# Table, signal and cross-term sums by accumulating transfers, the last 64 channels on both partition halves, and the squares' doublings moved into the transform rows

## The chip, the cores and the metric

The kernel runs on one core of a Trainium2 chip. The core has five engines, each with a queue of its own that it works off in order: TensorE (PE, matmuls and, overlapped with them, weight loads, PEld), VectorE (DVE), ScalarE (ACT), GpSimd (POOL) and SyncE (SP, which here does nothing but issue transfers). Sixteen DMA engines carry the transfers. The time is device microseconds of one execution.

## The reference

Two independent blocks, whose outputs are concatenated along the channels (S = L = 2048, D = 448):

```python
# A: linear attention, 16 heads of 28
q, k, v = split(x @ wqkv)
pq = einsum("bhsd,hdf->bhsf", q, w_phi); pk = einsum("bhsd,hdf->bhsf", k, w_phi)
phi_q = concat(softmax(pq), softmax(-pq)); phi_k = concat(softmax(pk), softmax(-pk))
kv = einsum("bhsf,bhsd->bhfd", phi_k, v); z = phi_k.sum(s)
o = einsum(phi_q, kv) / (einsum(phi_q, z) + 1e-6);  a = o @ wo
# B: state-space convolution, 256 states a channel
dt = exp(log_dt); logdA = dt * (A_re + i A_im)
P = exp(logdA[:, :, None] * l);  K = einsum("dn,dnl,dn->dl", C, P, dt * B).real
b = irfft(rfft(u padded) * rfft(K padded))[:L].astype(bf16) + u * Dskip
out = concat([a, b], axis=-1)
```

In the reference the positions `l` are rounded to bf16 (`l` takes the type of `A_re`), so K has only 640 different positions.

## The kernel before

**Order.** Every operation is recorded by a helper (`mul`, `add`, `sub` and `tt` at L177 for DVE, `af` at L198 for ACT, `copy`, `scaled` and `square` at L205, L208 and L211 for the engine that the list PICKS names, `mset` at L215 for GpSimd, `mms` at L220 for PE, `dma` at L240 and `dma_t` at L236 for SP) and issued afterwards in the order of a list of numbers, ORDER. PLACES gives each buffer its place in one large SBUF tile, so that buffers share bytes and an engine waits for whoever had the place before; SLOTS gives the PSUM banks. Each engine works in order. So one late operand stops all that is queued behind it on its engine.

**B, the kernel's coefficients.** The channels are worked off in four quarters `qt` of 112 channels (224 columns, QC, each with 128 states on the partitions in two halves of states). `tables(qt)` makes K at 640 positions as a product of 16 "high" and 40 "low" positions:

- `hi_tables` builds U_, C·B·exp at 16 high positions, by doubling: from 1 to 2, 4, 8, 16 entries, each a complex product. The last doubling multiplies 8 entries by the table PW[128].
- `damp` and `far` build W at 40 low positions. `far` has three steps by exp(256·...) (PW[256]; `step` with n = 7, 4, 4 rows) and two `squares` (rows at twice the position: re² − im², 2·re·im).
- `build_k` multiplies U_ (as weights, 32 columns at a time) with W on PE (80-wide matmuls), and `scatter_k` sends the result through DRAM (KTd) into the layout that the transform needs.

**B, the transforms.** `signal_spectrum(b)` for the two blocks b of 1024 rows: u's even rows and its odd rows are loaded as neighbours (`ua`), the odd ones reversed over the partitions by matmuls with a reversing matrix REV, then their sum and difference (1792 columns each) go through the matrix G1, and the spectra into DRAM (SUd, eight parts: four of block 0, four of block 1). `kernel_spectrum(qt)` multiplies rows F with K's table, and adds the two blocks' cross term by one more matmul of 112 columns for each part (NEG or ident). `conv(qt)` multiplies spectra on DVE (`prod`), sums them (`finish` on DVE, or `finish_pe` on PE) and transforms back (`inverse`).

**A.** `fold_weights` folds w_phi into the weights, `key_side` makes exp(±pk) and v for 16 pieces of 128 rows, `query_side` the outputs in four pieces of 512 rows. The contraction over 448 channels is four matmuls: three of 128 rows and one whose weights and data have 64 rows of zeros ahead of the last 64 channels (`Wp`, `WV` with memsets; `xT` loaded by transposing transfers).

The program runs both blocks together: tables(0), key_side, tables(1), then query sides, spectra, convolutions and the other tables in turn.

Of the kernel before, what the change touches and what calls it, by code (L numbers as in the profile page):

```python
# [14 lines left out]
PI = float(np.pi)  # L15

# [33 lines left out]
def _dft_tables():  # L50
# [24 lines left out]
    pid = np.zeros((128, 6, 128))  # L75
    for i, p in enumerate(ODD + [-1]):
        pid[np.arange(128), i, np.arange(128)] = p
    pid[np.arange(128), 5, 127 - np.arange(128)] = 1.0
# [41 lines left out]
def kernel(  # L120
# [23 lines left out]
    KTd = dram.tile([4, 3, 128, D_MODEL], BF16, name="KTd")  # L144
    SCd = dram.tile([4, 128, 128], BF16, name="SCd")
# [96 lines left out]
    PID = sb([128, 6, 128])  # L242
# [3 lines left out]
    REV = PID[:, 5, :]  # L246
# [12 lines left out]
    def load_x(i):  # L259
        for j in range(4):  # L260
            dma_t(xT[:, j, 512 * i:512 * i + 512], x2, 512 * i, 1, 512, XCOL[j])

    def row_pairs(row, a):
        rs = u2.ap[0][0]
        return bass.AP(tensor=u2.tensor, offset=u2[row + 128 * (1 - a), 0].offset,
                       ap=[[2 * rs, 64], [256 * rs, 4], [1, 2 * D_MODEL]])

    ua = [sb([128, 4, 2, D_MODEL]) for _ in range(2)]

    def load_u(b):  # L270
        for a in range(2):
            dma("S", ua[b][64 * a:64 * a + 64].rearrange("p t r d -> p t (r d)"), row_pairs(1024 * b, a))
# [19 lines left out]
    mset(WV[0:64, 3, :], 0.0)  # L292
    dma("S", WV[:, 0:3, :], A_wqkv[0:384, 2 * D_MODEL:].rearrange("(j p) n -> p j n", p=128))
    dma("S", WV[64:128, 3, :], A_wqkv[384:448, 2 * D_MODEL:])
# [6 lines left out]
    dma("S", G1, G_d)  # L301
    load_u(0)
# [42 lines left out]
    PW = {k: sb([128, 2, NCOL]) for k in (8, 16, 32, 64, 128, 256)}  # L345
    amp = {k: sb([128, NCOL], F32) for k in LOWP}
    cs = {k: sb([128, 2, NCOL], F32) for k in LOWP}
    q128, q256 = (sb([128, 2, NCOL], F32) for _ in range(2))
# [16 lines left out]
    for k in LOWP:  # L365
# [3 lines left out]
        if k == 128:  # L369
            copy(PW[128], q128)  # L370
    s2 = sb([128, 2, NCOL], F32)
    square(s2, q128)
    sub(q256[:, 0, :], s2[:, 0, :], s2[:, 1, :])
    stt(q256[:, 1, :], q128[:, 0, :], -2.0, q128[:, 1, :], ALU.mult, ALU.mult)
    copy(view(PW[256][:, 0, 0:1], [56, 32], [1, 2], [2, 28]), view(q256[:, 0, 0:1], [56, 32], [28, 2], [1, 28]))
# [8 lines left out]
    for w_ in Wp:  # L384
        mset(w_[0:64, 3, :], 0.0)

    def fold_weights(which):
# [6 lines left out]
        for jp in range(2):  # L394
            b = prog.banks(2)
            mms([(psum[64 * (j // 3):128, b[j % 2], 112 * c:112 * c + 112],
                  wT[:, which, c, 128 * j:min(128 * j + 128, D_MODEL)], BD[:, c, :],
                  dict(start=True, stop=True, tile_position=(0, 64 * (j // 3))))
                 for j in (2 * jp, 2 * jp + 1) for c in range(4)])
            if jp == 0:  # L400
                copy(Wp[which][:, 0:2, :], two(b))
            else:
                copy(Wp[which][:, 2, :], psum[:, b[0], 0:D_MODEL])
                copy(Wp[which][64:128, 3, :], psum[64:128, b[1], 0:D_MODEL])

    def signal_spectrum(b):
        ab = sb([128, 2, 4, D_MODEL])
        ur = sb([128, 4, D_MODEL])
        for tp in range(2):
            bs = prog.banks(2)  # L410
            mms([(psum[:, bs[k], 0:D_MODEL], REV, ua[b][:, 3 - 2 * tp - k, 1, :], dict(start=True, stop=True))
                 for k in range(2)])
            copy(ur[:, 2 * tp:2 * tp + 2, :], two(bs))
        add(ab[:, 0], ua[b][:, :, 0, :], ur)
        sub(ab[:, 1], ua[b][:, :, 0, :], ur)
        for cp in range(2):
            for st in range(2):
                k = 2 * cp + st
                sg = sb([128, 4, 4, 112])
                for mp in range(2):  # L420
                    items = []
                    bs = prog.banks(2)
                    for k2 in range(2):
                        mt = 2 * mp + k2
                        items += acc(psum[:, bs[k2], 0:D_MODEL],
                                     [(G1[:, cp, jt, 128 * mt:128 * mt + 128], ab[:, cp ^ st, jt, :])
                                      for jt in range(4)])
                    mms(items)
                    copy(sg[:, :, 2 * mp:2 * mp + 2, :].rearrange("p g k x -> p k g x"),
                         two(bs).rearrange("p k (g x) -> p k g x", g=4))  # L430
                dma("S", SUd[:, :, 4 * b + k, :].rearrange("g p x -> p g x"), sg.rearrange("p g k x -> p g (k x)"))
# [63 lines left out]
    def damp(W, A, T, qt, x0, w):  # L495
        scaled(A[:, 2:21:3, x0:x0 + w], A[:, 1:20:3, x0:x0 + w], -1.0)
        for part in (1, 0):
            copy(view(W[:, part, 1, x0:x0 + 1], [56, w // 56], [2, 28], [1, 2]),
                 view(PW[8][:, part, qt * QC + x0:qt * QC + x0 + 1], [56, w // 56], [1, 28], [28, 2]))
            mul(view(W[:, part, 2, x0:x0 + 1], [2 * QC, 7], [QC, 2], [1, w]),  # L500
                view(A[:, 0, x0:x0 + 1], [3 * QC, 7], [(1 + part) * QC, 2], [1, w]),
                view(T[:, part, 0, x0:x0 + 1], [QC, 7], [0, 2], [1, w]))

    def far(W, qt, x0, w):
        def pw(i, n):
            return view(PW[256][:, i, qt * QC + x0:qt * QC + x0 + 1], [0, 2], [0, n], [1, w])

        def at(part, row, n):
            return view(W[:, part, row, x0:x0 + 1], [WS, 2], [QC, n], [1, w])

        def rows_(part, row, n):
            return view(W[:, part, row, x0:x0 + 1], [QC, n], [1, w])

        def step(s0, d0, n):
            t = sb([128, 2, n, w])
            mul(t, at(0, s0, n), pw(1, n))
            mul(at(0, d0, n), at(0, s0, n), pw(0, n))
            sub(rows_(0, d0, n), rows_(0, d0, n), t[:, 1])
            add(rows_(1, d0, n), rows_(1, d0, n), t[:, 0])

        def squares(s0, ka, kb, d0):
            def four(part, row, a, b):
                return view(W[:, part, row, x0:x0 + 1], [a * QC, 2], [b * QC, 2], [1, w])
            sq = [sb([128, 4, w]) for i in range(2)]
# [5 lines left out]
        copy(view(W[:, 0, 16, x0:x0 + 1], [WS, 2], [1, w]),  # L530
             PW[256][:, :, qt * QC + x0:qt * QC + x0 + w])
# [6 lines left out]
    def hi_tables(qt):  # L538
# [52 lines left out]
    def key_side():  # L591
        bK = prog.banks(1), prog.banks(1)
        for pr in range(8):
# [3 lines left out]
            for t in range(2):  # L597
                ts_ = slice(128 * (2 * pr + t), 128 * (2 * pr + t) + 128)
                (b4,), (b5,) = prog.banks(1), prog.banks(1)
                mms(acc(psum[:, b4, 0:D_MODEL], [(xT[:, dj, ts_], Wp[1][:, dj, :]) for dj in range(4)]))  # L600
                mms(acc(psum[:, b5, 0:D_MODEL], [(xT[:, dj, ts_], WV[:, dj, :]) for dj in range(4)]))
# [32 lines left out]
    def query_side(sc):  # L634
        EQ = sb([112, 2, 4, 512])
        SB = sb([112, 8, 512])
        for c in range(4):
# [278 lines left out]
```

## Time and profile before

| | us |
|---|---|
| runs of the kernel | 235.62, 239.13, 235.87 (median 235.87) |
| the profiled execution, span from first to last instruction | 233.5 |
| PE busy / idle in it | 208.1 / 25.4 |
| DVE busy | 216.8 |
| ACT busy | 183.9 |
| granted TensorE clock | 1.000 |

The profiled execution is told by its span alone; what lies around the span (2.4 us to the median of the runs) is not in the trace. A row of a group reads: line of the code, engine, operation, output and inputs with partitions x elements and type, count, then busy us in all, mean ns of one, and the idle time ahead of it with what ended it. Mean durations of rows that follow each other on one engine overlap a little, so that busy time divided by count is the lower of the two measures of what one costs in a stream.

### The profile page before, as it was taken

The page shows a single profiled execution, that of the slowest core. Times are in us where ns is not written, and L with a number is a line of the kernel's source. Part 1 is how long each engine was busy: PE and PEld are TensorE (multiplying, and loading weights), DVE is VectorE, ACT ScalarE, POOL GpSimd, SP SyncE. Part 2 cuts the span into 40 slices and gives each one's busy share as a digit, 9 for nine tenths or more (in the row PEclk, how much of TensorE's full clock was granted, in tenths as well). Part 3 has the DMA queues.
Part 4 walks back from the last instruction along what each step waited for, and adds up shares of the span by engine and source line. Part 5 has one row for each costly group of instructions (what it writes and reads, how often), then busy time and mean ns, then how long its engine had stood idle before and what let it go on. Part 6 is the DMA issues. An engine that isn't in the chain of part 4 may idle for free.

```text
span 233.5 us, 7103 instructions
## 1 busy us (share of the span) xinstructions
PE 208.1 (89%) x3044; PEld 152.8 (65%) x3044; DVE 216.8 (93%) x267; ACT 183.9 (79%) x321; POOL 4.6 (2%) x20
## 2 busy tenths in 40 slices
PE   1173899998999999999987999999999999999994
PEld 1161446564557655589765678885579968689993
DVE  1799999999999999989999979999999999999980
ACT  3999999999999999999998998698328451355331
POOL 4000000000000100000000000000000000000000
PEclk9999999999999999999999999999999999999999
DMA  5999910499239999826865899872696890489643
GB/s 154 237 218 272 151 37 1 167 150 235 71 59 190 147 176 257 152 71 155 206 156 144 99 255 225 226 114 61 70 368 131 199 277 10 63 185 242 121 100 81
DMA packets 81640, 36.40 MB, mean 156 GB/s; under 512 B 65480, under 2 KB 79688, under 8 KB 81224
## 3 DMA queue, kind: packets, MB, share of 16 engines
q1 hardware_dynamic: 81368, 35.71, 73.3%
q8 instruction: 24, 0.39, 0.7%
q10 hardware_dynamic: 240, 0.23, 0.3%
q14 instruction: 8, 0.07, 0.1%
HBM read 19.44 MB, written 8.62 MB: 120 GB/s over the span
## 4 chain that ended last, share of the span: by engine, by line
PE 51%; ACT 17%; DVE 13%; DMA 5%; issue 3%; SPq 0%; ACTq 0%
PE psum L220 51%; DVE sbuf L177 11%; ACT sbuf L198 8%; ACT sbuf L205 7%; DMA sbuf<-sbuf 3%; DMA sbuf<-KTd 2%; ACT L198 1%; DVE sbuf L205 1%; DVE sbuf L194 0%; ACT sbuf L211 0%; SPq L240 0%; DVE sbuf L212 0%; ACT sbuf L208 0%; DVE sbuf L208 0%; PE psum L230 0%
## 5 line engine op out<-in xcount | busy, mean ns | idle before, releaser
L220 PE MATMUL psum<-sbuf 128*128 128x112 bf16 (+9 forms) x3000 | 206.2, 252 | 21.4 <-ACT sbuf L205 7.8
L177 DVE TENSOR_TENSOR sbuf<-sbuf 128x896 bf16<-128x896 bf16 (+11 forms) x222 | 197.3, 956 | 7.2 <-ACT sbuf L198 4.3
L220 PEld LDWEIGHTS <-sbuf 128*128 128x128 bf16 (+3 forms) x3000 | 150.1, 114 | 75.3 <-issue 18.2
L205 ACT CAST sbuf<-psum 128x448 bf16<-128x448 f32 (+4 forms) x129 | 79.7, 672 | 38.0 <-PE psum L220 37.3
L198 ACT ACTIVATE sbuf<-psum 128x448 bf16<-128x448 f32 (+4 forms) x110 | 65.5, 721 | 0.5 <-PE psum L220 0.4
L211 ACT ACTIVATE sbuf<-sbuf 128x896 bf16<-128x896 bf16 x14 | 14.2, 1024 | 4.0 <-DVE sbuf L177 4.0
L198 ACT ACTIVATE sbuf<-psum,sbuf 128x896 f32<-128x896 f32 (+3 forms) x17 | 13.6, 835 | 0.0
L208 ACT ACTIVATE sbuf<-sbuf 128x896 bf16<-128x896 bf16 (+2 forms) x10 | 10.9, 1091 | 1.4 <-DVE sbuf L299 0.8
L198 ACT ACT_TABLE_LOAD x8 | 10.3, 1283 | 1.4 <-PEq L900 1.3
L205 ACT COPY sbuf<-sbuf 128x224 bf16<-128x224 bf16 (+2 forms) x18 | 8.9, 512 | 0.0
L205 DVE CAST sbuf<-psum 128x448 bf16<-128x448 f32 (+3 forms) x8 | 5.3, 690 | 2.3 <-PE psum L220 1.7
L215 POOL MEMSET sbuf<- 128x224 bf16 (+4 forms) x15 | 4.2, 314 | 153.3 <-PE psum L220 153.1
L205 ACT COPY sbuf<-psum 112x896 bf16<-112x896 bf16 (+2 forms) x13 | 6.8, 549 | 0.1
L177 DVE TENSOR_TENSOR sbuf<-psum,sbuf 128x448 bf16<-128x448 f32 (+3 forms) x12 | 5.1, 444 | 0.1
L194 DVE RECIPROCAL sbuf<-psum 128x64 bf16<-128x64 f32 x8 | 4.3, 546 | 0.4 <-ACT sbuf L198 0.3
L230 PEld LDWEIGHTS <-sbuf 112*112 112x112 bf16 (+1 forms) x44 | 3.1, 128 | 1.8 <-DVE sbuf L177 0.8
L230 PE MATMUL psum<-sbuf 112*112 112x112 bf16 (+1 forms) x44 | 3.6, 215 | 0.6 <-DVE sbuf L177 0.6
L212 DVE TENSOR_TENSOR sbuf<-sbuf 128x896 bf16<-128x896 bf16 (+1 forms) x3 | 3.3, 1087 | 0.0
L194 DVE RECIPROCAL sbuf<-sbuf 128x64 f32<-128x64 f32 x4 | 2.2, 545 | 0.0
L189 DVE SCALAR_TENSOR_TENSOR sbuf<-sbuf 128x64 f32<-128x64 f32 (+1 forms) x5 | 2.0, 393 | 0.0
L205 ACT CAST sbuf<-sbuf 128x1792 bf16<-128x1792 f32 x1 | 1.8, 1814 | 0.0
L208 DVE TENSOR_SCALAR sbuf<-sbuf 128x1568 bf16<-128x1568 bf16 (+1 forms) x3 | 1.6, 538 | 0.0
(8 smaller groups left out, 2.1 us busy)
## 6 DMA issues: line engine op xcount, KB each, us to landing
SUd<-sbuf SPq DMA_DIRECT2D x8, 448.0 KB
sbuf<-SCd SPq DMA_DIRECT2D x16, 224.0 KB
sbuf<-SUd SPq DMA_DIRECT2D x4, 896.0 KB
sbuf<-const SPq DMA_DIRECT2D x3, 1024.0 KB
sbuf<-const SPq DMA_DIRECT2D x8, 384.0 KB
sbuf<-in_B_u_dram SPq DMA_DIRECT2D x4, 448.0 KB
out_dram<-sbuf SPq DMA_DIRECT2D x4, 448.0 KB
out_dram<-sbuf SPq DMA_DIRECT2D x16, 112.0 KB
```

The lines of the kernel that those rows point to most:

```text
L177: prog.add("V", lambda: nc.vector.tensor_tensor(out=o, in0=a, in1=b, op=op))
L189: prog.add("V", lambda: nc.vector.scalar_tensor_tensor(out=o, in0=a, scalar=s, in1=b, op0=op0, op1=op1))
L194: nc.vector.reciprocal(o, a)
L198: prog.add("A", lambda: nc.scalar.activation(o, a, fn, **kw))
L205: either(lambda: nc.scalar.copy(o, a), lambda: nc.vector.tensor_copy(o, a))
L208: either(lambda: nc.scalar.activation(o, a, ACT.Copy, scale=s), lambda: nc.vector.tensor_scalar_mul(o, a, s))
L211: either(lambda: nc.scalar.activation(o, a, ACT.Square), lambda: nc.vector.tensor_tensor(out=o, in0=a, in1=a, op=ALU.mult))
L212: lambda: nc.vector.tensor_tensor(out=o, in0=a, in1=a, op=ALU.mult))
L215: prog.add("G", lambda: nc.gpsimd.memset(o, v))
L220: nc.tensor.matmul(o, lhsT=l, rhs=r, **kw)
L230: nc.tensor.transpose(o, i, idn)
```

## The change

**Accumulating transfers.** A new helper issues transfers from GpSimd that add their source to their destination, each split in two:

```diff
+    def dma_add(o, i):
+        parts = ((o[:, 0:2], i[:, 0:2]), (o[:, 2:4], i[:, 2:4])) if len(o.shape) == 3 else ((o, i),)
+        prog.add("G", lambda: [nc.gpsimd.dma_start(out=a, in_=b, accum_op=ALU.add) for a, b in parts])
```

There are 28 of them, in three uses. First, U_'s last doubling (four transfers in each quarter, two for each half of the table that `build_k` reads; N128 is −im of PW[128]):

```diff
-        for i, o in ((1, t), (0, U_[:, :, 8:16])):
-            times(o, U_[:, :, 0:8], PW[128][:, i, cols], 16)
-        sub(U_[:, :, 8:16, 0, :], U_[:, :, 8:16, 0, :], t[:, :, :, 1, :])
-        add(U_[:, :, 8:16, 1, :], U_[:, :, 8:16, 1, :], t[:, :, :, 0, :])
+        def part_times(i, z):
+            mul(t[:, :, :, i, :], U_[:, :, 0:8, 1 - i, :],
+                z.rearrange("p (s x) -> p s x", x=28).unsqueeze(2).to_broadcast([128, 8, 8, 28]))
+        part_times(0, N128[:, cols])
+        part_times(1, PW[128][:, 1, cols])
+        times(U_[:, :, 8:16], U_[:, :, 0:8], PW[128][:, 0, cols], 16)
+        for c in range(2):
+            dma_add(*(v.rearrange("p s n i x -> p s (n i x)") for v in (U_[:, 4 * c:4 * c + 4, 8:16], t[:, 4 * c:4 * c + 4])))
```

Second, the signal's sum, and third, block 1's spectra, which are added in DRAM to block 0's with the cross term's sign; block 0's are written twice by SP, and the 64 matmuls of the cross term go. u's odd rows are now turned by a transfer from DRAM to DRAM (URd) and loaded from there, which replaces REV:

```diff
-            mms([(psum[:, bs[k], 0:D_MODEL], REV, ua[b][:, 3 - 2 * tp - k, 1, :], dict(start=True, stop=True))
-                 for k in range(2)])
-            copy(ur[:, 2 * tp:2 * tp + 2, :], two(bs))
-        add(ab[:, 0], ua[b][:, :, 0, :], ur)
-        sub(ab[:, 1], ua[b][:, :, 0, :], ur)
+        ab = (ue[b], sb([128, 4, D_MODEL]))
+        sub(ab[1], ue[b], uo[b])
+        dma_add(ue[b], uo[b])
...
+                if b == 0:
+                    dma("S", SUd[:, :, k, :].rearrange("g p x -> p g x"), sg_)
+                    dma("S", SUd[:, :, 6 - 2 * cp + st, :].rearrange("g p x -> p g x"), sg_)
+                else:
+                    dma_add(SUd[:, :, 4 + k, :].rearrange("g p x -> p g x"), sg_)
...
-        if b == 1:
-            items[-1][3]["stop"] = False
-            items.append((view(o[:, 0:1], [14, 8], [7, 2], [1, 7]), (NEG, ident)[cp],
-                          view(sk0(1 - cp, m)[:, 0:1], [14, 8], [1, 2], [2, 7]), dict(start=False, stop=True)))
```

**The last 64 channels.** The channels 384 to 447 stand on partitions 64 to 127 for one matmul and, copied by SP, on 0 to 63 for another. Two sums that use them are issued together: three full matmuls each, then the two of 64 rows, in the upper and the lower half of the array. `key_side` pairs its two outputs (448 columns), `query_side` two pieces of 512 columns; `fold_weights` makes the doubled rows, and the zeros' memsets go.

```diff
+    def beside(two_):
+        whole = [(o, l, r, dict(start=(i == 0), stop=False)) for o, ps_ in two_ for i, (l, r) in enumerate(ps_[:3])]
+        return whole + [(o, ps_[3][0][64 * k:64 * k + 64], ps_[3][1][64 * k:64 * k + 64],
+                         dict(start=False, stop=True, tile_position=(64 * k, 0))) for k, (o, ps_) in enumerate(two_)]
```

**Far steps and squares.** PW[256] becomes P256 with three parts (−im, im, re), so that a step is two multiplies and one sum of the full width; the squares run on ACT with a factor of √½ and without the doubling of re·im, so the rows come out halved; GROWN puts factors of 2 and 8 into the transform's rows F instead.

```diff
+            mul(t, view(W[:, 1, s0, 0:1], [-WS, 2], [1, n * QC]),
+                view(P256[:, 0, qt * QC:qt * QC + 1], [NCOL, 2], [0, n], [1, QC]))
+            mul(dst, src, view(P256[:, 2, qt * QC:qt * QC + 1], [0, 2], [0, n], [1, QC]))
+            add(dst, dst, t)
...
-                square(sq[i].rearrange("p (a b) x -> p a b x", a=2), four(i, s0, ka, kb))
+                af(sq[i].rearrange("p (a b) x -> p a b x", a=2), four(i, s0, ka, kb), ACT.Square, scale=HALF)
             mul(four(1, d0, 2, 1), four(0, s0, ka, kb), four(1, s0, ka, kb))
-            scaled(rows_(1, d0, 4), rows_(1, d0, 4), 2.0)
...
+GROWN = [1, 1, 1, 2, 8]
...
+            F[blk, kt, r] += GROWN[kt] * np.stack([even.real, odd.real, even.imag, odd.imag])
```

In `conv`, the sum of the two products takes a subtract and an add of 1792 columns each in place of an add of 3584, where it runs on DVE; in `query_side` the score multiply is one of 4096 columns in place of two of 2048.

**The lists.** ORDER, PLACES, SLOTS and PICKS are written anew, a number for each operation:

```diff
-    "1 2 0 3 27 41 42 44 35 30 43 5 58 59 61 204 62 49 7 52 50 53 60 51 6 54 8 45 57 46 9 55 70 56 47 48 71 4 172 72 "
+    "1 0 2 3 49 50 52 68 38 53 55 5 8 70 7 51 66 56 65 9 57 60 67 6 63 40 62 4 61 64 58 79 78 54 71 72 59 43 174 80 "
```

DVE at the end of table 0, before. The shapes name the work: 128x8x448 and 128x3584 are the two multiplies of U_'s last doubling, 128x8x8x28 its subtract and add, and 128x2x896 and 128x896 are steps and squares of `far`.

```order
L177 TENSOR_TENSOR sbuf<-sbuf 128x8x448
L177 TENSOR_TENSOR sbuf<-sbuf 128x8x2x28 x2
L177 TENSOR_TENSOR sbuf<-sbuf 128x2x896
L177 TENSOR_TENSOR sbuf<-sbuf 128x3584
L177 TENSOR_TENSOR sbuf<-sbuf 128x1792 x3
L177 TENSOR_TENSOR sbuf<-sbuf 128x8x8x28 x2
L177 TENSOR_TENSOR sbuf<-sbuf 128x896 x2
L177 TENSOR_TENSOR sbuf<-sbuf 128x8x4x28 x2
```

And after; 128x64x28 are the two multiplies by the imaginary part, and 128x8x28 and 128x8x2x28 belong to table 1's first doublings.

```order
L178 TENSOR_TENSOR sbuf<-sbuf 128x64x28
L178 TENSOR_TENSOR sbuf<-sbuf 128x8x28
L178 TENSOR_TENSOR sbuf<-sbuf 128x8x448
L178 TENSOR_TENSOR sbuf<-sbuf 128x64x28
L178 TENSOR_TENSOR sbuf<-sbuf 128x8x28
L178 TENSOR_TENSOR sbuf<-sbuf 128x896 x4
L178 TENSOR_TENSOR sbuf<-sbuf 128x8x2x28
L178 TENSOR_TENSOR sbuf<-sbuf 128x2x896
L178 TENSOR_TENSOR sbuf<-sbuf 128x8x2x28
L178 TENSOR_TENSOR sbuf<-sbuf 128x1792 x3
L178 TENSOR_TENSOR sbuf<-sbuf 128x2x896
```

The multiplies of the last doubling now come closer to each other, nothing of U_ is left on DVE behind them, and the rest of `far`, mixed with table 1's rows, stands between them and the end of W.

GpSimd's queue, the stretch in which its memsets stood before:

```order
L215 MEMSET sbuf 64x448
L215 MEMSET sbuf 112x448
L215 MEMSET sbuf 128x224 x2
L215 MEMSET sbuf 128x128
L215 MEMSET sbuf 64x448
L215 MEMSET sbuf 128x224
```

And after, where `sbuf<-sbuf 128x896` are signal sums, `SUd<-sbuf` block 1's spectra and `sbuf<-sbuf 128x2x448` U_'s sums (the first four are table 0's, the second table 1's):

```order
L250 DMA sbuf<-sbuf 128x896 x2
L216 MEMSET sbuf 112x448
L216 MEMSET sbuf 128x224
L250 DMA sbuf<-sbuf 128x896 x2
L216 MEMSET sbuf 128x224
L250 DMA SUd<-sbuf 128x2x448 x6
L250 DMA sbuf<-sbuf 128x2x448 x4
L216 MEMSET sbuf 128x128
L250 DMA SUd<-sbuf 128x2x448 x2
L250 DMA sbuf<-sbuf 128x2x448 x4
```

Table 0's four transfers stand behind the signal sums and six of the eight transfers into SUd.

More of the change, by code (lines that the diff above doesn't have):

```diff
@@ L301 @@
     dma("S", G1, G_d)
+    turn_u()
     load_u(0)
@@ L504, in far @@
[L504 to L509, printed above, removed]
+            copy(view(W[:, part, 1, 0:1], [56, 4], [2, 28], [1, 2]),
+                 view(PW[8][:, part, qt * QC:qt * QC + 1], [56, 4], [1, 28], [28, 2]))
+            mul(view(W[:, part, 2, 0:1], [2 * QC, 7], [QC, 2], [1, QC]),
+                view(A[:, 0, 0:1], [3 * QC, 7], [(1 + part) * QC, 2], [1, QC]),
+                view(T[:, part, 0, 0:1], [QC, 7], [0, 2], [1, QC]))
@@ L511, in rows_, with far @@
+    def far(W, qt):
         def rows_(part, row, n):
-            return view(W[:, part, row, x0:x0 + 1], [QC, n], [1, w])
+            return view(W[:, part, row, 0:1], [QC, n], [1, QC])
         def step(s0, d0, n):
[L515 to L519, printed above, removed]
+            t = sb([128, 2, n, QC])
+            src, dst = (view(W[:, 0, r, 0:1], [WS, 2], [1, n * QC]) for r in (s0, d0))
+            mul(t, view(W[:, 1, s0, 0:1], [-WS, 2], [1, n * QC]),
+                view(P256[:, 0, qt * QC:qt * QC + 1], [NCOL, 2], [0, n], [1, QC]))
+            mul(dst, src, view(P256[:, 2, qt * QC:qt * QC + 1], [0, 2], [0, n], [1, QC]))
+            add(dst, dst, t)
@@ L527, in squares @@
             mul(four(1, d0, 2, 1), four(0, s0, ka, kb), four(1, s0, ka, kb))
-            scaled(rows_(1, d0, 4), rows_(1, d0, 4), 2.0)
             sub(rows_(0, d0, 4), sq[0], sq[1])
-        copy(view(W[:, 0, 16, x0:x0 + 1], [WS, 2], [1, w]),
-             PW[256][:, :, qt * QC + x0:qt * QC + x0 + w])
+        for part in range(2):
+            copy(W[:, part, 16, :], P256[:, 2 - part, qt * QC:qt * QC + QC])
         step(1, 17, 7)
@@ L796, in tables @@
         mset(W[:, 1, 0, :], 0.0)
-        for x0, w in SPLIT[qt]:
-            damp(W, A, T, qt, x0, w)
-            far(W, qt, x0, w)
-            for c in range(x0 // 112, (x0 + w) // 112):
-                build_k(W, U_, TS, c)
+        damp(W, A, T, qt)
+        far(W, qt)
+        for c in range(2):
+            build_k(W, U_, TS, c)
         scatter_k(qt, TS, KT[qt])
```

135 lines of the change are left out of this document (68 added, 67 removed), and 100 rows, old and new, of tables (ORDER, PLACES, SLOTS).

## The prediction

> **What bounds the kernel now.** I first read the page's busy totals and its DMA queue, then the chain that ended last by engine, and then cut the span into stages, since totals average over stages with different limits.
>
> ```profile
> PE 208.1 (89%) x3044; PEld 152.8 (65%) x3044; DVE 216.8 (93%) x267; ACT 183.9 (79%) x321; POOL 4.6 (2%) x20
> q1 hardware_dynamic: 81368, 35.71, 73.3%
> PE 51%; ACT 17%; DVE 13%; DMA 5%; issue 3%; SPq 0%; ACTq 0%
> ```
>
> VectorE (DVE) is busiest, yet half of the chain is TensorE (PE). The stages say why (columns: length, busy time and count of PE, weight loads, DVE, ACT, POOL, then granted clock, DMA share, GB/s):
>
> ```profile
> 0.00:30.00 30.00, 14.02 (x90) 9.64 (x91) 23.29 (x26) 26.12 (x36) 2.51 (x12) 1.00 0.95 204
> 30.00:130.00 100.00, 94.02 (x1216) 62.09 (x1214) 98.41 (x136) 98.68 (x176) 1.58 (x6) 1.00 0.68 138
> 130.00:230.00 100.00, 100.00 (x1742) 81.09 (x1740) 95.08 (x107) 58.59 (x110) 0.51 (x2) 1.00 0.77 162
> ```
>
> To 30 us the kernel loads and starts. From 30 to 130 us DVE and ACT are both full and PE nearly. From 130 us on PE has no gap while ACT idles 41 us. The chain agrees, and shows two transfers that PE waited for:
>
> ```profile
> 93.61 6.15 DMA sbuf<-sbuf
> ...
> 119.11 5.06 DMA sbuf<-KTd
> ...
> 129.69 31.20 PE psum L220 x553
> ...
> 160.94 12.11 PE psum L220 x64
> 173.11 56.97 PE psum L220 x1087
> ```
>
> So DVE or ACT work removed pays before 130 us; behind it only matmuls pay.
>
> **The change, part by part.** DVE's own rows:
>
> ```profile
> L177 DVE TENSOR_TENSOR sbuf<-sbuf 128x3584 bf16<-128x3584 bf16 x23 | 46.1, 2020 | 0.1
> L177 DVE TENSOR_TENSOR sbuf<-sbuf 128x1792 bf16<-128x1792 bf16 x44 | 46.1, 1081 | 0.0
> L177 DVE TENSOR_TENSOR sbuf<-sbuf 128x3136 bf16<-128x3136 bf16 x16 | 28.2, 1783 | 0.4 <-ACT sbuf L205 0.4
> L177 DVE TENSOR_TENSOR sbuf<-sbuf 128x896 bf16<-128x896 bf16 x74 | 43.0, 617 | 2.3 <-ACT sbuf L211 1.8
> L177 DVE TENSOR_TENSOR sbuf<-sbuf 128x1568 bf16<-128x1568 bf16 x8 | 7.5, 957 | 0.0
> L177 DVE TENSOR_TENSOR sbuf<-sbuf 112x2048 bf16<-112x2048 bf16 x8 | 9.5, 1218 | 0.0
> L205 DVE CAST sbuf<-psum 128x448 bf16<-128x448 f32 x5 | 3.1, 638 | 2.3 <-PE psum L220 1.7 <-ACT sbuf L198 0.6
> L205 DVE CAST sbuf<-sbuf 128x1792 bf16<-128x1792 f32 x1 | 1.2, 1184 | 0.0
> L208 DVE TENSOR_SCALAR sbuf<-sbuf 128x896 bf16<-128x896 bf16 x1 | 0.4, 386 | 0.0
> L177 DVE TENSOR_TENSOR sbuf<-sbuf 128x224 bf16<-128x224 bf16 x8 | 2.0, 267 | 0.0
> L177 DVE TENSOR_TENSOR sbuf<-sbuf 128x448 bf16<-128x448 bf16 x16 | 5.8, 383 | 0.0
> ```
>
> - Last doubling of U: before, two multiplies of 3584 and a subtract and an add of 1792 (6.20 us); after, one multiply of 3584 and two of 1792 (4.18), the sum going to a transfer. Four tables: −8.1.
> - The steps of `far`: at n=7 two multiplies of 3136 and two sums of 1568 (5.48) become three rows of 3136 (5.35); at n=4, 2×1.081+2×.617=3.40 becomes 3×1.081=3.24. Four and eight times: −1.8.
> - Squares: two squares and a doubling leave DVE (2×.617+.386): −1.6. Signal sums: two of four rows of 1792 go: −2.2. The conv sum becomes two of 1792 for one of 3584, twice: +.3. The score multiply becomes 4 of 4096; from the slope between the rows of 1792 and 3584, (2.020−1.081)/1792, I estimate 2.29 each: −.6.
> - Copies picked anew: four more casts of 448 (+2.6) less one each of 240, 320 and 896 (.553, .696 and 1.084 by the next fence: −2.3); one cast of 1792 from ACT (+1.2); 17 small copies and scalings, 16 to 448 long, which have no row on DVE. The nearest are .267 and .386; bounds .1 and .39 each give +1.7 to +6.6, and I take .2, +3.4, as a one-source copy is not above the cheapest two-source row.
>
> ```profile
> L205 DVE CAST sbuf<-psum 128x896 bf16<-128x896 f32 x1 | 1.1, 1084 | 0.0
> L205 DVE CAST sbuf<-psum 128x320 bf16<-128x320 f32 x1 | 0.7, 696 | 0.0
> L205 DVE CAST sbuf<-psum 128x240 bf16<-128x240 f32 x1 | 0.6, 553 | 0.0
> L205 ACT COPY sbuf<-sbuf 128x448 bf16<-128x448 bf16 x8 | 5.0, 623 | 0.0
> L208 ACT ACTIVATE sbuf<-sbuf 128x896 bf16<-128x896 bf16 x7 | 7.2, 1032 | 0.6 <-DVE sbuf L177 0.5
> L205 ACT CAST sbuf<-psum 128x448 bf16<-128x448 f32 x82 | 43.9, 586 | 25.2 <-PE psum L220 24.6 <-DVE sbuf L177 0.4
> ```
>
> DVE in sum: −9.1, so 207.7. ACT loses eight copies of 448 (−5.0), four sbuf rows of 896 (−4.1), eight casts of 448 (−4.7) and some smaller: 14 to 15 us, most of it before 130 us, where it shares the bound.
>
> PE's rows and the one place of before that has half-width matmuls:
>
> ```profile
> L220 PE MATMUL psum<-sbuf 128*128 128x448 bf16 x328 | 66.9, 358 | 4.2 <-ACT sbuf L205 3.8
> L220 PE MATMUL psum<-sbuf 128*128 128x112 bf16 x1064 | 55.4, 213 | 4.0 <-ACT sbuf L205 2.6 <-DMA sbuf<-KTd 1.5
> 57.37 0.36 PE L220 MATMUL psum<-sbuf 112*128 112x112 bf16 x4 [0.76 <-ACT sbuf L205]
> 57.42 0.53 PE L220 MATMUL psum<-sbuf 112*128 112x112 bf16 x5
> 57.66 0.68 PE L220 MATMUL psum<-sbuf 112*64 112x112 bf16 x5
> ```
>
> In a stream a matmul of 448 takes 66.9/328=.204 us and one of 112 takes .052 (55.4/1064). The 64 correction matmuls go from the spectra, all behind the gather that lands at 119.11+5.06=124.2: −3.3 in the stage where PE is full. Eight wider folds cost +.4 and the eight REV matmuls give 1.6, both early.
>
> The last 64 channels: 24 pairs (16 in `key_side`, 8 in `query_side`) turn two full matmuls with zero rows into two of 64 rows that may run together. If they fully do, −24×.204=−4.9. Against it stands the change of tile shape: in the fence starts are .05 apart (57.37, 57.42; the fourth near 57.52) and the first half-width one starts at 57.66, .09 late. Into and out of it, .19 a pair: with no overlap at all +4.6. I take 0, as the gain (.204) and two changes (.19) cancel. The Trainium skill (TensorEngine Tiling (Array Packing), Performance Considerations) says that tiles operate independently and that a change of tiling mode drains TensorE; the .09 above agrees with the drain, and by independence without a drain the sum would be 4.9 lower. PE in sum: 208.1−3.3+.4−1.6=203.6.
>
> The accumulating transfers. Nothing in before issues one from GpSimd. In `build_k`, PE waits for U from the transfer and W from DVE. The cover is DVE's work between U's last multiply and W's last row. By the order (front part) that is for table 0 a 224, four 896, two 448, and five rows of 1792: .27+2.47+.77+5.41=8.9 us; counted alike 34, 15 and 10 for tables 1 to 3. A half table is two transfers of 128 x 2 x 448, each 229,376 bytes. Nearest landings: the gather, 5.06, and the transposes, 6.15; two halves one behind the other would be 10 to 12, overlapped 5 to 6. I take 6, as the four are independent: nothing waits. Behind a PE that waits stand key side, folds and ACT's evictions. The Trainium skill (DMA: Bandwidth & Descriptors, Anatomy of one DMA) fits 2.0 us + bytes/436e3 for such a transfer, so an estimate of 2.5 us; no run here shows it.
>
> Issue order: table 0's transfers stand on POOL behind six SUd accumulates, and those behind SP's block-0 writes; SP is late already:
>
> ```profile
> SPq L240 <- ACT sbuf L205: 36.6, 16, 12.1
> 29.69 7.73 PE L220 MATMUL psum<-sbuf 128*128 128x448 bf16 x40 [0.94 <-ACT sbuf L205]
> 72.89 3.31 PE L220 MATMUL psum<-sbuf 128*32 128x80 bf16 x164
> ```
>
> SP's longest wait there is 12.1 us, and the first signal matmuls stand 43 us ahead of table 0's `build_k` (the 80-wide ones from 72.89), so I count no wait. SP gets G1 behind the turned copy of u (one DRAM-to-DRAM transfer, 0.92 MB) and a wait for it. PE idles 16 us in the first 30, so 2 to 3 us of that are hidden; without that cover they shift everything. Signal sums by transfer: PE needs ue about one landing (5 to 6) after the subtract, which runs the odd part first; in exchange eight REV matmuls and four copies leave the head.
>
> DMA bytes: 28×.229=6.4, turned u .92, row copies .26, so +7.6 MB on 35.71; at the same rate 73% becomes 89%. It bounds nothing by itself.
>
> **The sum by stage.** Behind 130 us: −3.3. Before it, DVE holds two tables and all signal sums: half of −8.1, −1.8 and −1.6, all of −2.2, some +3 of copies, so about −5; I take −4 of it, since PE at 94 us is close behind. Bounds 0 and −8 (ACT's relief in full). 233.5−7.3=226.2 of span; the median of the runs stands 2.4 above this span (235.87), so 228.5.
>
> **Rivals.**
> - *Same.* The first 130 us give nothing: the ready times are set by SP, the SUd chain or another transfer like the 6.15 and 5.06 above. PE's late −3.3, with about −1 of the head, remains: 229.2+2.4=231.6, up to 235.9 if waits take all of it. For it: this stage's three engines are within 5 us of each other. Against: both of the two fullest get lighter, ACT by much.
> - *More.* Pairs overlap without a drain and ACT's relief counts in full: −4.9 and −4 more: 219.6.
> - *Slower.* U's sums land late, GpSimd being held up by DVE. If each of four issues of a table waits out a 3584 multiply (2.02) and two landings of 5.06 follow, U is ready 18.2 us behind its multiply. PE then waits 9.3, 3.2 and 8.2 at tables 0, 2 and 3: 228.5+20.7=249.2. With L for the landing and covers of 8.9, 15 and 10, waits eat the gain past 2% (2.7 us) from L=10.8, and from L=15.3 it is slower by over 2%. The Trainium skill (SBUF — State Buffer, SBUF: two separate sides) has this: DVE in a two-port mode locks GpSimd out of the shared port, so that it cannot write descriptors, and it advises against such transfers beside DVE. By the letter two-source rows aren't in it. What before shows of GpSimd beside a full DVE speaks against:
>
> ```profile
> 77.49 1.07 POOL L215 MEMSET sbuf<- 128x224 bf16 x4 [74.32 <-PE psum L220]
> ```
>
> Four writes in 1.07 us, while DVE's rows are .6 to 2 us long: none was held for one. But these are not transfers, and DMA share is near full for long stretches.
> - *Not done as said.* Accumulates that run one by one (28×6.15=172 us on one queue) would still fit the span but not table 0's cover: 4×6.15=24.6, more than the rival above; it is counted there.
>
> **How the numbers follow.** Forecast .50, more .08, same .20, slower .22. A difference under 2% (231.2 to 240.6) is what I take for no change. Forecast's own range: copies and pairs ±3, 224 to 232. Faster .57: forecast and more, less .01 for the forecast's upper edge, which goes to same, .21; slower .22. The range from 221 to 244 takes in the forecast, the same case, half of the case of more and the lower third of the slower one: .5+.2+.04+.07, about .8.
>
> **What would show it.** Right: DVE near 208 and ACT near 169 busy; PE full from about 123 us; no PE wait on a transfer into U. Wrong: PE or weight loads waiting on `DMA sbuf<-sbuf` ahead of the 80-wide matmuls; PE busy above 206 with idle time between pairs of 64 rows (overlap absent); ACT waiting on SUd's transfers; a first signal matmul later than 29.7 us.

## The result, and the profile after

| | us |
|---|---|
| before, median of 4 runs | 236.26 |
| after, median of 4 runs | 289.79 (288.28 to 296.24) |
| ratio | 1.224, 95% interval 1.215 to 1.233 |
| profiled execution after | 288.28, of it span 286.5 |

The change makes the kernel 53 us slower. The ratio goes by the fast runs; the one after at 296.24 us was a slow one. From the page after, the busy totals, the two kinds of DMA queue and the chain by engine:

```profile
PE 213.9 (75%) x2980; PEld 151.8 (53%) x2980; DVE 211.7 (74%) x264; ACT 173.6 (61%) x297; POOL 36.3 (13%) x45
q1 hardware_dynamic: 83816, 36.86, 60.3%
q0 software_dynamic: 7104, 6.42, 17.3%
PE 36%; issue 19%; DMA 12%; DVE 12%; SPq 8%; ACT 7%; POOL 5%; DVEq 0%; ACTq 0%; POOLq 0%
```

The work got less, though not by as much as announced (DVE −5 in place of −9, ACT −10 in place of −14 to −15), but no engine is full any more: PE idles 286.5−213.9=72.6 us in place of 25.4, and is busy 5.8 us longer although it has 64 matmuls fewer. "Issue" (19%) and POOL (5%) are new on the chain. The stages, cut as for the kernel before:

```profile
0.00:30.00 30.00, 10.09 (x72) 7.61 (x73) 19.67 (x24) 20.71 (x26) 3.30 (x10) 0.92 0.89 196
30.00:130.00 100.00, 71.05 (x658) 38.52 (x657) 67.33 (x86) 65.78 (x112) 20.36 (x19) 0.85 0.78 139
130.00:230.00 100.00, 89.66 (x1478) 68.88 (x1476) 87.03 (x115) 72.28 (x131) 8.81 (x12) 0.97 0.81 165
```

From 30 to 130 us PE, DVE and ACT all stand still for about 30 us (PE: 658 matmuls in place of 1216), and the granted clock falls to 0.85. From 130 us on PE has holes. Where they all wait is told by GpSimd's queue (rows: start, duration, what, idle time before it and what ended it):

```profile
25.34 1.93 POOL L250 DMA_DIRECT2D sbuf<-sbuf  x2 [24.00 <-DVE sbuf L178]
...
39.89 1.75 POOL L250 DMA_DIRECT2D sbuf<-sbuf  x2 [11.91 <-DVE sbuf L178]
...
53.26 1.22 POOL L250 DMA_DIRECT2D SUd<-sbuf  x1 [11.32 <-ACT sbuf L206]
60.89 1.21 POOL L250 DMA_DIRECT2D SUd<-sbuf  x1 [6.42 <-issue]
65.58 1.19 POOL L250 DMA_DIRECT2D SUd<-sbuf  x1 [3.48 <-issue]
...
79.61 1.22 POOL L250 DMA_DIRECT2D SUd<-sbuf  x1 [3.47 <-issue]
84.30 1.20 POOL L250 DMA_DIRECT2D sbuf<-sbuf  x1 [3.48 <-issue]
89.23 1.22 POOL L250 DMA_DIRECT2D sbuf<-sbuf  x1 [3.73 <-issue]
93.10 1.20 POOL L250 DMA_DIRECT2D sbuf<-sbuf  x1 [2.65 <-issue]
97.78 1.21 POOL L250 DMA_DIRECT2D sbuf<-sbuf  x1 [3.49 <-issue]
...
132.69 1.21 POOL L250 DMA_DIRECT2D sbuf<-sbuf  x1 [5.51 <-PE psum L221]
```

Each transfer of U or SUd takes 1.2 us to issue, and then GpSimd mostly stands still for some 3.5 us (2.6 to 6.7) with no wait that the profile shows ahead of the next one ("issue"). Of the transfers' semaphores, GpSimd waits there only for those of transfers that had landed long before. Six transfers into SUd go by from 53 to 84 us, and only then table 0's four into U. The median from issue to landing is in the transfers' list:

```profile
sbuf<-sbuf POOLq DMA_DIRECT2D x20, 224.0 KB, 5.2
SUd<-sbuf POOLq DMA_DIRECT2D x8, 224.0 KB, 4.4
```

A landing of 4.4 us and the next issue 4.7 us behind the last one (60.89, 65.58): one transfer is under way at a time. The first into SUd, issued at 53.26, took 7.3 us to land, and the one behind it went out 7.6 us later: the gap follows the landing, and the next issue comes 0.3 us behind it. Each of these transfers has 256 pieces of 896 bytes, two for each partition. Only the four signal sums, 128 pieces of 1792 bytes each and so the same 229 KB, went out in pairs (25.34 and 39.89). PE's rows show the price:

```profile
75.72 5.09 PE L221 MATMUL psum<-sbuf 128*128 128x448 bf16 x16 [6.59 <-ACT sbuf L206]
89.01 0.49 PE L221 MATMUL psum<-sbuf 128*32 128x80 bf16 x8 [8.20 <-issue]
92.83 3.69 PE L221 MATMUL psum<-sbuf 128*32 128x80 bf16 x104 [3.32 <-DMA sbuf<-sbuf]
97.51 0.37 PE L221 MATMUL psum<-sbuf 128*32 128x80 bf16 x8 [1.00 <-DMA sbuf<-sbuf]
103.83 1.03 PE L221 MATMUL psum<-sbuf 128*32 128x80 bf16 x24 [5.95 <-DMA sbuf<-sbuf]
```

`build_k` of table 0 starts or goes on at 89.01, 92.83, 97.51 and 103.83, each time when another of the four transfers has landed, the last one (issued at 97.78) 6.0 us behind its issue; in the kernel before it began at 72.89 and ran through without a gap. Over all four tables, PE idles 33.3 us ahead of these matmuls in place of nothing (before, then after):

```profile
L220 PE MATMUL psum<-sbuf 128*32 128x80 bf16 x896 | 18.3, 258 | 0.0
L221 PE MATMUL psum<-sbuf 128*32 128x80 bf16 x896 | 27.0, 333 | 33.3 <-DMA sbuf<-sbuf 12.3 <-POOL sbuf L216 11.1 <-issue 9.9
```

The 11.1 us put down to POOL L216 are two waits for memsets of W, which stand in GpSimd's queue behind U's transfers and come late with them.

### The profile page after: what moved, and what is told of

Read it like the earlier page. It is cut to its first block, busy times and chain, and to the rows that moved or that the text cites. A ratio compares the mean times of both kernels' runs of the same rounds, so it can differ in the third digit from the quotient of the medians.

```text
span 286.5 us, 7015 instructions
## 1 busy us (share of the span) xinstructions
PE 213.9 (75%) x2980; PEld 151.8 (53%) x2980; DVE 211.7 (74%) x264; ACT 173.6 (61%) x297; POOL 36.3 (13%) x45
## 3 DMA queue, kind: packets, MB, share of 16 engines
q0 software_dynamic: 7104, 6.42, 17.3%
## 4 chain that ended last, share of the span: by engine, by line
PE 36%; issue 19%; DMA 12%; DVE 12%; SPq 8%; ACT 7%; POOL 5%; DVEq 0%; ACTq 0%; POOLq 0%
PE psum L221 36%; DVE sbuf L178 10%; DMA sbuf<-sbuf 7%; SPq L246 5%; ACT sbuf L199 4%; DMA sbuf<-SCd 3%; POOL SUd L250 3%; SPq L242 2%; POOL sbuf L250 2%; ACT sbuf L206 2%; DVE sbuf L206 2%; DMA sbuf<-in_B_u_dram 2%; DMA sbuf<-in_B_log_dt_dram 1%; ACT L199 1%; DVE sbuf L209 0%
## 5 line engine op out<-in xcount | busy, mean ns | idle before, releaser
L221 PE MATMUL psum<-sbuf 128*32 128x80 bf16 (+8 forms) x2936 | 211.9, 277 | 69.0 <-ACT sbuf L206 16.8
L178 DVE TENSOR_TENSOR sbuf<-sbuf 128x1792 bf16<-128x1792 bf16 (+10 forms) x202 | 189.9, 991 | 25.6 <-DMA sbuf<-SCd 10.0
L206 ACT CAST sbuf<-psum 128x448 bf16<-128x448 f32 (+4 forms) x118 | 69.1, 633 | 93.9 <-PE psum L221 83.4
L250 POOL DMA_DIRECT2D sbuf<-sbuf x20 | 23.0, 1181 | 146.2 <-DVE sbuf L178 51.1
L206 DVE COPY sbuf<-sbuf 128x224 bf16<-128x224 bf16 (+2 forms) x16 | 3.8, 240 | 30.2 <-PE psum L221 30.2
L199 ACT ACTIVATE sbuf<-sbuf 128x896 bf16<-128x896 bf16 (+1 forms) x17 | 14.9, 915 | 5.4 <-DVE sbuf L178 2.7
L250 POOL DMA_DIRECT2D SUd<-sbuf x8 | 9.7, 1206 | 40.1 <-issue 28.8
L199 ACT ACTIVATE sbuf<-psum,sbuf 128x896 f32<-128x896 f32 (+3 forms) x17 | 13.4, 814 | 0.5 <-PE psum L221 0.5
L206 DVE CAST sbuf<-psum 128x448 bf16<-128x448 f32 x9 | 5.6, 630 | 7.3 <-PE psum L221 5.4
L216 POOL MEMSET sbuf<- 128x224 bf16 (+3 forms) x12 | 6.6, 707 | 17.0 <-PE psum L221 16.7
L209 ACT ACTIVATE sbuf<-sbuf 128x1568 bf16<-128x1568 bf16 (+1 forms) x3 | 4.1, 1370 | 0.0
```

Source lines behind the costliest of these rows:

```text
L178: prog.add("V", lambda: nc.vector.tensor_tensor(out=o, in0=a, in1=b, op=op))
L199: prog.add("A", lambda: nc.scalar.activation(o, a, fn, **kw))
L206: either(lambda: nc.scalar.copy(o, a), lambda: nc.vector.tensor_copy(o, a))
L209: either(lambda: nc.scalar.activation(o, a, ACT.Copy, scale=s), lambda: nc.vector.tensor_scalar_mul(o, a, s))
L216: prog.add("G", lambda: nc.gpsimd.memset(o, v))
L221: nc.tensor.matmul(o, lhsT=l, rhs=r, **kw)
```

## The experiments

Three theories were set against each other. A: GpSimd sends these transfers one at a time, so U's sums come late. B: the new lists and loads lose time by themselves. C: DVE holds GpSimd up while it runs. Ratios are to the kernel before, run beside each experiment, with 95% intervals; an experiment has two runs where nothing else is said.

**U's sums back on DVE.**

```diff
-            dma_add(*(v.rearrange("p s n i x -> p s (n i x)") for v in (U_[:, 4 * c:4 * c + 4, 8:16], t[:, 4 * c:4 * c + 4])))
+            o, i = (v.rearrange("p s n i x -> p s (n i x)") for v in (U_[:, 4 * c:4 * c + 4, 8:16], t[:, 4 * c:4 * c + 4]))
+            add(o, o, i)
```

> The changed kernel with U's sixteen sums back on DVE (two adds of 1792 for each table, at the same places of the list); signal and SUd sums stay transfers. Theory A (GpSimd sends transfers of 2 x 128 pieces one at a time, each from the landing of the one ahead, so U's sums come 20 to 40 us late): PE's waits for transfers into U go, 25 to 45 us, against +8.6 us of DVE; 240 to 255 us. Rival B (the new lists and places lose the time by themselves, the transfers are only where it shows): over 275. Rival C (DVE holds GpSimd up while it runs): as A for this run.

Measured: 257.79 us, ratio 1.093 (1.072 to 1.114). 32 us come back, at a cost of 7.4 us more of DVE (219.1 busy); a little above A's range, so A holds for most of it and something is left.

**U's transfers ahead of SUd's.** Only the list is changed, numbers 166, 156 and 161 behind 198 (three of the sums into SUd then take what has been written into their sources' places meanwhile).

> The changed kernel with table 0's four transfers into U ahead of the six SUd transfers in GpSimd's queue, nothing else moved. Theory A: each of the six costs 4.6 us of waiting ahead of table 0 (53 to 84 us in the profile after); U's own four stay one by one, and its product is ready near 68 us, so table 0 comes 16 to 20 us earlier; 268 to 276 us. B: 285 or more. C: the four wait for DVE's rows all the same, and gaps between them vary with DVE's work.

Measured: 286.57 us, ratio 1.215 (1.192 to 1.238). By its size this is B's figure, not A's; the queue shows why A expected too much:

```profile
64.56 1.21 POOL L250 DMA_DIRECT2D sbuf<-sbuf  x1 [22.39 <-DVE sbuf L178]
68.45 1.20 POOL L250 DMA_DIRECT2D sbuf<-sbuf  x1 [2.68 <-issue]
72.32 1.34 POOL L250 DMA_DIRECT2D sbuf<-sbuf  x1 [2.67 <-issue]
76.90 1.20 POOL L250 DMA_DIRECT2D sbuf<-sbuf  x1 [3.24 <-issue]
...
113.59 1.22 POOL L250 DMA_DIRECT2D SUd<-sbuf  x1 [3.45 <-issue]
119.96 1.20 POOL L250 DMA_DIRECT2D sbuf<-sbuf  x1 [5.15 <-issue]
...
138.28 1.21 POOL L250 DMA_DIRECT2D sbuf<-sbuf  x1 [4.51 <-PE psum L221]
```

Table 0's four go out 20 us earlier, but now SUd's eight stand ahead of table 1's, whose last goes out at 138.28 (132.69 in the changed kernel). The queue is busy without a break from 64 to 138 us: its order decides which table waits, its rate how long all of them do together.

**Transfers of 128 pieces.** Bytes the same, twice as many transfers (the signal sums are cut too, from two of 128 pieces of 1792 bytes to four of 896).

```diff
-        parts = ((o[:, 0:2], i[:, 0:2]), (o[:, 2:4], i[:, 2:4])) if len(o.shape) == 3 else ((o, i),)
+        parts = [(o[:, k], i[:, k]) for k in range(4)]
```

> The changed kernel with each accumulating transfer into U and SUd cut into two of 128 pieces (48 in place of 24; bytes the same, pieces of 896 bytes). Theory A1 (the limit is on pieces in flight, so that 256 and 256 don't fit but 128 and 128 do, as the signal sums of 128 pieces went out .7 us apart): issues 0.7 to 1.2 us apart at least by twos; a table's sums land in 10 to 14 us in place of 20; 255 to 275 us. Theory A2 (an accumulating transfer into this layout always goes alone): 48 in series at 4 us each, slower than 300. B: 285 to 295.

Measured: 264.15 us, ratio 1.120 (1.092 to 1.148): 26 us come back by cutting the same bytes into more transfers. GpSimd's rows:

```profile
25.49 2.79 POOL L250 DMA_DIRECT2D sbuf<-sbuf  x3 [24.15 <-DVE sbuf L178]
30.12 0.88 POOL L250 DMA_DIRECT2D sbuf<-sbuf  x1 [1.83 <-issue]
...
53.45 2.65 POOL L250 DMA_DIRECT2D SUd<-sbuf  x3 [8.49 <-ACT sbuf L206]
59.97 2.67 POOL L250 DMA_DIRECT2D SUd<-sbuf  x3 [3.86 <-issue]
```

Three go out in a row and the fourth waits: 3 x 128 = 384 pieces are taken at once and 4 x 128 = 512 are not, as 2 x 256 = 512 were not. A1 holds and A2 falls. It isn't the bytes: the pairs of signal sums in the changed kernel had 2 x 229 KB under way, as much as two transfers into U, which were never under way together.

**The kernel before with U's sums alone by transfers**, and the same with 128 pieces (the second diff on top of the first):

```diff
-        sub(U_[:, :, 8:16, 0, :], U_[:, :, 8:16, 0, :], t[:, :, :, 1, :])
-        add(U_[:, :, 8:16, 1, :], U_[:, :, 8:16, 1, :], t[:, :, :, 0, :])
+        for c in range(2):
+            dma_add(*(v.rearrange("p s n i x -> p s (n i x)") for v in (U_[:, 4 * c:4 * c + 4, 8:16], t[:, 4 * c:4 * c + 4])))
...
-        parts = ((o[:, 0:2], i[:, 0:2]), (o[:, 2:4], i[:, 2:4]))
+        parts = [(o[:, k], i[:, k]) for k in range(4)]
```

> The kernel before with only U's last sums by transfers, four for each table in the places of its subtract and add (the products are added without their exchange of parts and sign). DVE loses 8.6 us. Theory A: the second to fourth transfer of a table start from the landing of the one ahead though no semaphore holds them; U's second half is 18 us behind its multiply, PE waits 5 to 12 us at each of the tables that have no cover; 245 to 265 us. B: within 5 us of the kernel before, 230 to 240. C: issue gaps vary between 1 and 5 us with DVE's rows.

> As e5 (the kernel before with U's last sums by transfers, 275.6 us), with eight transfers of 128 pieces a table in place of four of 256 (the products again without exchange of parts and sign). If at most 384 to 511 pieces are in flight, three go at once and a table's eight land about 10 to 12 us behind the first issue in place of 16 to 25: 248 to 262 us. If the loss were DVE's and ACT's order around U, 272 to 278.

Measured: 275.63 us, ratio 1.168 (1.147 to 1.190), and 258.17 us, ratio 1.090 (1.081 to 1.100). One part of the change, in the old lists and with only memsets beside it in GpSimd's queue, loses 39 us, more than A gave it; nearly half of that (17 us) comes back with smaller transfers. From the first of the two, GpSimd and PE:

```profile
66.16 1.34 POOL L244 DMA_DIRECT2D sbuf<-sbuf  x1 [62.98 <-DVE sbuf L177]
70.60 1.23 POOL L244 DMA_DIRECT2D sbuf<-sbuf  x1 [3.10 <-issue]
74.87 1.21 POOL L244 DMA_DIRECT2D sbuf<-sbuf  x1 [3.04 <-issue]
81.34 1.21 POOL L244 DMA_DIRECT2D sbuf<-sbuf  x1 [5.26 <-issue]
```

```profile
81.16 0.50 PE L220 MATMUL psum<-sbuf 128*32 128x80 bf16 x8 [8.13 <-DMA sbuf<-sbuf]
85.47 6.60 PE L220 MATMUL psum<-sbuf 128*32 128x80 bf16 x216 [3.81 <-DMA sbuf<-sbuf]
```

The four follow one another 4.3 to 6.5 us apart, and no instruction's wait stands ahead of the last three. The sums are complete at 85.47, 19 us behind the first issue; their cover there was shorter than in the changed kernel.

**SUd by plain writes, and no adding transfers at all.**

```diff
-                    dma_add(SUd[:, :, 4 + k, :].rearrange("g p x -> p g x"), sg_)
+                    dma("S", SUd[:, :, 4 + k, :].rearrange("g p x -> p g x"), sg_)
...
-        dma_add(ue[b], uo[b])
+        add(ue[b], ue[b], uo[b])
```

> As e1 (257.8 us), and block 1's spectra go into SUd by plain writes of SP instead of adding transfers, so that the cross term between the blocks is left out and its 64 matmuls are not put back; only the four signal sums are adding transfers. Theory A (what is left of the loss in e1 is again GpSimd's one-at-a-time queue: SUd's eight from 53 to 99 us, for whose landing ACT waited 6.3 us): 243 to 250 us. Rival B (the new lists, built for other landings, lose it in SP's and DVE's order): within 3 us of e1, 255 to 260.

> As e6, and the signal sums on DVE too (two adds of 1792): no adding transfer at all; turned u, row halves, far steps, squares and the new lists stay. A: 240 to 250 us, the signal sums' landing (5 to 7.6 us behind their issue at 25 us) being the last thing ahead of the first signal matmuls. B: 250 to 260, and the waits that stay are SP's (late transposes of u at the end, 223 to 240 us in e1) and DVE's. If the parts that stay were worth what was forecast of them, it would be 230 or less.

Measured: 251.83 us, ratio 1.063 (1.054 to 1.073), and 255.18 us, ratio 1.077 (1.068 to 1.087). SUd's transfers cost some 6 us by the medians, though the interval of the first ratio just touches that of the run with U's sums on DVE. What the signal sums cost as transfers these two don't show; on DVE they are dearer by 3 us (ranges of two runs each: 250.67 to 253.0, 254.32 to 256.04). Without any adding transfer the time is still far from 230: B has a part.

**Sums left out.** In the changed kernel all 28 transfers are taken away with nothing in their place, or only U's sixteen.

```diff
-            dma_add(*(v.rearrange("p s n i x -> p s (n i x)") for v in (U_[:, 4 * c:4 * c + 4, 8:16], t[:, 4 * c:4 * c + 4])))
+            prog.add("G", lambda: None)
```

> The changed kernel with all 28 adding transfers left out and nothing in their place: U's last cross terms, the signals' sums and the sums into SUd are missing from what is computed. This is the change as if its transfers cost and delayed nothing. Theory A (the loss is the transfers' landing and nothing else): the forecast's own sum, 226 to 232 us. Rival B (the new order of the lists and the loads at the start lose time also without any transfer): 240 to 250; PE's busy time then is near 204 and its idle time stays above 35.

> The changed kernel with the sixteen transfers of U's sums left out (U lacks its last cross terms), signal and SUd sums staying as they are. A: the difference to e10 is what the twelve others cost, the difference to the changed kernel (289.8 us) what U's cost: 40 to 55 us. B: 245 to 260.

Measured: 247.51 us, ratio 1.049 (1.040 to 1.057), and 251.57 us, ratio 1.066 (1.058 to 1.074). So U's transfers cost 289.8−251.6=38 us, about what they cost alone in the old lists (39), the twelve others 4, and the change with transfers that cost nothing is still 11 us slower than the kernel before. Its stages (all sums left out):

```profile
0.00:30.00 30.00, 10.43 (x71) 7.82 (x72) 19.32 (x24) 20.34 (x26) 1.53 (x9) 1.00 0.80 195
30.00:130.00 100.00, 92.72 (x1175) 56.09 (x1174) 95.73 (x133) 93.66 (x164) 1.55 (x6) 1.00 0.65 146
130.00:230.00 100.00, 91.80 (x1471) 70.93 (x1470) 85.97 (x98) 55.58 (x102) 0.51 (x2) 0.95 0.73 142
```

In the first 30 us DVE gets 4.0 and ACT 5.8 us less done than in the kernel before, but they also have less to do, and at 130 us they have only 1.1 and 0.5 us more left than there. PE has fallen behind: its busy time in the profile is 208.3 us, so 208.3−10.4−92.7=105.2 us are left at 130 us, where 208.1−14.0−94.0=100.1 were. From there to 230 us PE, once without a gap, idles 8.2 us at a clock of 0.95. These 5.1 and 8.2 us make up 13.3 of the 13.4 by which this span (246.9) is longer.

**Single parts in the old lists.** Squares with the doublings in F:

```diff
+                af(sq[i].rearrange("p (a b) x -> p a b x", a=2), four(i, s0, ka, kb), ACT.Square, scale=HALF)
...
-            scaled(rows_(1, d0, 4), rows_(1, d0, 4), 2.0)
+            prog.add(prog.pick(), lambda: None)
```

> The kernel before with one part of the change alone: squares on ACT with a factor of sqrt(1/2), the doublings dropped and put into the rows F. DVE -1.6 us, ACT -5.2 us in all, half of it in the first 130 us where both are full. If that stage is bound by them as my prediction says, 232.5 to 235; if its ready times are set elsewhere, no difference that can be measured, 235 to 236.5.

Measured: 241.27 us, ratio 1.016 (1.008 to 1.023), from six runs: slower with less work, by less than 2% but clear of 1, and outside both ranges. Two of table 0's squares went from DVE to ACT, and DVE's waits for ACT's rows of `af` and `square` grew from 4.3+1.8=6.1 to 9.7 us (before, then this run, where all the squares are `af`'s and its line is L200):

```profile
DVE sbuf L177 <- ACT sbuf L198: 4.3, 1, 4.3
DVE sbuf L177 <- ACT sbuf L211: 1.8, 2, 1.2
DVE sbuf L179 <- ACT sbuf L200: 9.7, 5, 4.2
```

With table 0's squares left where they were (its half is put in by a scaling on ACT and one on DVE in place of the doublings):

```diff
+                if qt == 0:
+                    square(sq[i].rearrange("p (a b) x -> p a b x", a=2), four(i, s0, ka, kb))
```

> As e9 (the kernel before with the doublings put into the rows F, 241.3 us), with table 0's squares left on the engines where they were (DVE waited there 9.7 us for ACT in e9, 4.3 before); table 0's factor of one half takes the place of its doublings, so only tables 1 to 3 lose work: six ACT rows of 1.03 us, nothing added anywhere. If e9 lost its time by that wait alone: 233 to 236. If any row taken out of the lists moves the others apart, whichever it is: 238 to 241 again.

Measured: 237.68 us, ratio 1.0016 (0.997 to 1.006), from twelve runs: no difference, between the two cases. The wait is back at 5.1 us, and the loss went with it; and six rows less of ACT, 4.9 us of its busy time (183.9 to 179.0), are worth nothing.

```profile
DVE sbuf L179 <- ACT sbuf L200: 5.1, 2, 4.3
```

SUd's sums alone, the matmuls of the cross term gone:

```diff
+                        if row in written:
+                            for a in range(0, 4, 2):
+                                nc.gpsimd.dma_start(out=o_[:, a:a + 2], in_=sg_[:, a:a + 2], accum_op=ALU.add)
+                        else:
+                            nc.sync.dma_start(out=o_, in_=sg_)
```

> The kernel before with one part of the change alone: SUd's sums by eight adding transfers of 256 pieces (for each part the earlier of the two blocks is written plainly, the later one added), the cross term's 64 matmuls gone, signs as in the change. Nobody waits for these transfers within 40 us. PE's stage from 130 us on is full, so the 3.3 us of matmuls that I took out of the sum show: 231 to 234 us if that step was right; 235 to 240 if the sources' buffers, held 20 to 40 us longer, make ACT or PE wait.

Measured: 240.82 us, ratio 1.017 (1.011 to 1.023), from six runs, a little above the upper case: the matmuls taken from PE do not show. The run puts eight adding transfers in their place, and whether these, the buffers that they hold or something else takes the time isn't shown.

No version that was run beats the kernel before.

## Why the prediction was wrong, point by point

- **The step that failed first**: "I take 6, as the four are independent: nothing waits." No semaphore holds the four, and they still went one by one. U's product was ready at 63.7 us (DVE's last multiply; the run with U first issued at 64.56), the cover ended 8.5 us later as forecast, and the sums were complete at 103.8: 40 us in place of 6, of which 20 are SUd's transfers ahead in the queue and 20 its own four at 4.9. U's sixteen transfers are 38 of the 53 us lost, shown by leaving them out.
- **The rival that had the mechanism** was "not done as said": transfers that run one by one, 4 x 6.15 = 24.6 us for a table. I priced the table by itself and put it into the slower case, without working out its time: with the covers of 8.9, 15 and 10 us it gives waits of 15.7, 9.6 and 14.6 and so 268 us, above the slower rival's 249 and outside my range. What was not added either is that 24 such transfers share one queue, 24 x 4.7 = 113 us of it as an estimate by the step from 60.89 to 65.58, and that in this order table 0 is delayed by SUd's six and table 1 by SUd's last two.
- **"SP is late already ... so I count no wait"** had the right queue and the wrong end of it: no wait of GpSimd ahead of U's transfers ended at one of SP's landings, the transfers ahead were the wait. ACT also waited 7.0 us for one of SUd's transfers to land, a sign that I had named.
- **The slower rival**, GpSimd held up by DVE, had the sign and not the cause. GpSimd's issue of 256 pieces took 1.19 to 1.22 us, all 24 times, beside a full DVE and beside one that stood still (from 77.9 to 108.1 us), and the gap behind it ends with a landing, 0.3 us before the next issue; theory C finds no support in any run. The rule of the Trainium skill that I named there (SBUF — State Buffer, SBUF: two separate sides) isn't contradicted, since nearly all of DVE's rows have two sources, but it isn't what happened here.
- **The sum by stage** failed in its two gains as well. "Behind 130 us: −3.3": the matmuls went, but in the new order PE isn't full there (91.8 of 100 us with all sums left out), and in the old order the same cut, with eight adding transfers for it, gave +4. "I take −4 of it": six ACT rows less gave nothing. Both took a stage full of work for one bound by the amount of it. The other 11 us of loss stand as 5 us that PE is behind at 130 us and as the holes of 8 us after it; which move of the lists or loads makes each was not tried, and stays open.
- **Row halves: right.** Taken as 0. (The rule of the Trainium skill on the drain stands in TensorEngine Tiling (Array Packing) under Key Properties, not under Performance Considerations.) After, in the one pair that was read: the last full matmul ahead of it starts at 63.87, both halves at 64.15, the next full one .30 later, while full ones follow each other .19 apart; the pair takes .58−.19=.39 us, as much as two full ones (.38, or .41 at .204 each). The halves run side by side, and the two changes of shape cost what that saves:

```profile
63.87 0.65 PE L221 MATMUL psum<-sbuf 128*128 128x448 bf16 x3
64.15 0.66 PE L221 MATMUL psum<-sbuf 64*128 64x448 bf16 x3
```

- **Work**: DVE 211.7 us (207.7 forecast), ACT 173.6 (169). The small copies were near the estimate: .24 us for 224, .27 for 448, .2 taken. The steps of `far`, −1.8 in the sum, gave nothing: their rows of 3136 and 1792 took 7.3 and 8.5 us more, those of 1568 and 896 7.5 and 8.1 less. PE 213.9 (203.6): of the 10.3 us too little, 8.7 stand in `build_k`'s matmuls, which took 27.0 us in place of 18.3. They start behind the waits, and the granted clock there (89.0 to 97.9 us) was 0.55, against 0.911 on the mean after and 1.000 before; the sum had no term for the clock.

## What to carry to other kernels

Before work is handed to transfers, find out how many the issuing queue holds under way at once; where it is one, multiply the landing by the number that share the queue: a single transfer's landing is no price for four of them in a row. Transfers of fewer pieces may go out together where larger ones of the same bytes go singly. In a kernel ordered by hand, work removed from a full engine pays only where the order that hangs on it is looked at again: here −5 us of ACT gave 0, and −3.3 us of PE, with eight adding transfers for it, gave +4.

## What the runs showed of the hardware

- Adding transfers from GpSimd have a limit on what is under way that no semaphore shows: two of 256 pieces never overlapped, three of 128 did, the fourth waited for the first landing. So the limit lies between 384 and 511 pieces. Bytes are ruled out by the pairs of signal sums (2 x 229 KB in 2 x 128 pieces); the queue's 7104 packets are the 24 x 256 + 4 x 128 pieces and 16 more for each of the 28 transfers, and whether these count too wasn't separated.
- A single one of 229 KB lands in 4.4 (SUd) and 5.2 us (SBUF, the signal pairs among them) by the medians, from 3.5 to 7.6 us; the issue of 256 pieces is 1.2 of it. An estimate from the fit of the Trainium skill (DMA: Bandwidth & Descriptors, Anatomy of one DMA) was 2.5 us; the measurement decides.
- The granted clock was lower where PE stood still for long: 0.85 in the stage from 30 to 130 us with 71 us of PE work, 1.00 there in the kernel before with 94. The share of work alone doesn't give it: in the first 30 us of the kernel before, PE worked 14.0 us and the clock was 1.00.
